# Converting the weights w1 and w2 in chunks of 1024 columns in place of 512

## The chip, the cores and the metric

The kernel runs on one core of a Trainium2 chip. The metric is the time of one execution on the device in microseconds, as the median of several runs. The engines are TensorE (PE in the profile, PEld for its weight loads), VectorE (DVE), ScalarE (ACT), GpSimd (POOL) and SyncE (SP), which here does nothing but issue transfers.

## The reference

Three blocks run one after the other on a batch of two sequences of 768 tokens and 512 features (8 heads of 64):

```python
mask = q_bucket[:, :, :, None] == k_bucket[:, :, None, :]   # buckets: signs of q @ proj, k @ proj
scores = np.where(mask, scale * q @ k.T, -1e9)
x = softmax(scores) @ v                                     # heads joined to (B, 768, 512)

u = x + np.real(np.fft.fft(np.fft.fft(x, axis=1), axis=2))
x = u + np.maximum(layernorm(u) @ w_ch1, 0.0) @ w_ch2       # 512 -> 2048 -> 512

theta = x @ w_theta
y = w_tok_r @ (x * cos(theta)) + w_tok_i @ (x * sin(theta))
u = x + y
out = u + np.maximum(u @ w_ch, 0.0)
```

The weights w_ch1, w_ch2, w_theta, w_tok and w_ch arrive as pairs of 32-bit words of float64 values.

## The kernel before

Products are formed from a high and a low part of each operand, so every weight must be converted on the core: from float64 words to float32, then into a high part (float16 for w1 and w2, fp32r for the others) and a low part, the difference.

`from_f64` does the first half for one chunk. It takes a buffer `r` from a ring of NCV = 3 in the pool `cv`, issues the load on SP, and makes float32 words of the two halves: two ScalarE operations (`r` with the bias `chalf`, then `r` again) and one VectorE operation that shifts and joins them. `conv16` (w1 and w2, 8192 columns each) and `conv32` (the theta and channel matrices `wth` and `wch`, 2048 columns each) go over the columns in chunks of CN = 512, and add two operations: ScalarE copies the chunk into the high part (`w1h`, `w2h`), GpSimd subtracts it for the low part (`w1l`, `w2l`). A buffer is free for the next load when the low part is made. `conv_tok` does the same for the token matrices in chunks of TH = 384 columns, and passes that width to `from_f64`.

The order on each engine is set by a planner: each piece of work gets a due time in us by `at(...)` (`timed` raises it by a step per chunk: w1s for w1, w2s for w2), and the planner lays the instructions in order of due time as they come ready in its own model. Each engine then runs its queue in that order. `take(cw1, k0)` and `take(cw1, k1 - k0)` part the chunks of w1 into three groups, which may start after different gates: the end of the first attention's transposes (`cv`), the first norm (`ln0`), and its last step.

Around the change the work is: the attention of the first batch (to about 136 us, order written by hand), its Fourier transform `Fft(0)` with the copies into `u` and the first norm (to about 213 us), beside it the attention of the second batch (tiles `stk`, `pss`, `p`, `pt`, `x`, 48 steps to about 375 us), and the MLP of the first batch (`psm` from `w1h`, `w1l`, then `w2h`, `w2l`). The first three chunks of w1 are loaded at the start, since their buffers are free; all other loads wait for a buffer. The same SP queue issues the transposes of the attention (`pt`, `x`). After the second attention come the transform, norm and MLP of the second batch, then theta, the token products and the channel product of both.

Of the kernel before, what the change touches and what calls it, by code (L numbers as in the profile page):

```python
# [33 lines left out]
def f(t):  # L34
    return t.bitcast(F32)
# [35 lines left out]
def fused_kernel(ctx, tc, A, out):  # L71
    nc = tc.nc
# [5 lines left out]
    def mk(p, shape, dt, tag, **kw):  # L78
        return p.tile(shape, dt, tag=tag, name=tag, **kw)
# [7 lines left out]
    def stt(eng, out, in0, in1, op, scale=1.0):  # L87
        if eng is V:
            return V.scalar_tensor_tensor(out=out, in0=in0, scalar=scale, in1=in1, op0=ALU.mult, op1=op)
        assert scale == 1.0  # L90
        return eng.tensor_tensor(out=out, in0=in0, in1=in1, op=op)

    T = dict(
        pet='dpd', dup=1, c2=0, c0=46, cx=0, wm=6, gf=1, o2=0, xs=1, sb=2, al=[['p', 2], ['p2', 3], ['pt', 3]], cs='v', g0=1,
        lg=[[0, 2], [2, 4], [4, 6]], ub=2, pace0=1.6, lead=60, f0=50.0, w1=60.0, w1s=1.0, b1=115, pace1=2.6,
        w2=100.0, w2s=1.0, m0=170.0, f1=190.0, th=240.0, m1=290.0, z0=330.0, wt=300.0, n0=8, n1=16, k0=12, k1=16, c1=46,
        ne=42, es=150, ld='ss', lc='s', ps=[[0, 3], [0, 5], [1, 0], [1, 5]])
    P3 = ((0, 0), (0, 1), (1, 0))

# [58 lines left out]
    x_t, u_t = {}, {}  # L158


    CN, NCV = 512, 3

    def from_f64(src, scale=1.0, n=CN):
        p = cvs[turn["cv"] % len(cvs)]
        turn["cv"] += 1
        r = mk(p, [128, 2 * CN], U32, "r64", bufs=NCV if p is cv_p else None)
        r = r[:, 0:2 * n]
        {"s": SY, "a": AC, "p": PL}[T["lc"]].dma_start(out=r, in_=src.bitcast(U32))
        lo, hi = r[:, 0:2 * n:2], r[:, 1:2 * n:2]

        AC.activation(out=lo, in_=lo, func=AF.Relu, scale=2.0 ** -29 * (1 - 2.0 ** -20), bias=c_half)

        AC.activation(out=f(hi), in_=f(hi), func=AF.Prelu, scale=scale * 2.0 ** -112, alpha=2.0 ** 32)
        V.scalar_tensor_tensor(out=lo, in0=hi, scalar=3, in1=lo, op0=ALU.logical_shift_left, op1=ALU.bitwise_or)
        return f(lo)
# [7 lines left out]
            yield  # L183

    def conv32(src, n, hi, lo):
        for i in range(n // CN):
            c = slice(CN * i, CN * i + CN)
            w = from_f64(src[:, c])
            AC.activation(out=hi[:, c], in_=w, func=AF.Copy)
            stt(PL, lo[:, c], w, f(hi[:, c]), ALU.subtract)  # L190
            yield
# [565 lines left out]
    w1, w2 = {}, {}  # L757
# [152 lines left out]
    h1, l1, c1, c2 = (ev(k) for k in ("aapap", "p", "p", "p"))  # L910
# [79 lines left out]

    wth = [mk(th_p, [128, 4, DM], F32R, f"wth{k}") for k in "hl"]
    timed(conv32(A["wth"], 4 * DM, flat3(wth[0]), flat3(wth[1])), T["th"], 2)
    zz = lambda p, tag: mk(p, [128, NT, DM], F32R, tag)
    z_t[0] = [[zz(x_p, "x"), zz(zb_p, "za")], [zz(zb_p, "zb"), zz(zb_p, "zc")]]
# [31 lines left out]
    def operands(p, q):  # L1026
        ks = mk(q, [128, 2, 4, TH], F32R, "ks" if q is xt_p else "u1")
        return mk(p, [128, 4, TH], F32, "xt"), ks[:, 0], ks[:, 1]
# [8 lines left out]
    k0 = operands(xt_p, xt_p)  # L1037
# [4 lines left out]
    wc_p = pool("wc", 1, side="right")  # L1042
    wch = [mk(wc_p, [128, 4, DM], F32R, f"wch{k}") for k in "hl"]
    timed(conv32(A["wch"], 4 * DM, flat3(wch[0]), flat3(wch[1])), t0 + 22, 1)
    xt1_p = pool("xt1", 1, side="right")
    k1 = operands(xt1_p, u1_p)
# [5 lines left out]
    k0 = operands(xt_p, xt_p)  # L1052
# [4 lines left out]
    k1 = operands(xt1_p, u1_p)  # L1057
# [107 lines left out]
```

## Time and profile before

| | |
|---|---|
| median of 3 runs | 739.85 us (738.78 to 742.93) |
| the profiled execution | 742.76 us |
| its span, first to last instruction | 741.0 us |
| mean granted clock of TensorE in it | 0.969 |
| busy: PE, PEld, DVE, ACT, POOL | 665.2, 508.2, 399.7, 376.5, 371.2 us |

Busy times are of the whole span; what one stage is worth is read from that stage. All rows below are of this one execution, and its own time is 2.91 us above the median.

A row of the windows gives a stretch and its length, for PE, PEld, DVE, ACT and POOL the busy us and, as (x...), the instructions, and then the granted clock (PEclk, 1.00 is full), the mean busy share of the 16 DMA engines and GB/s. A group by shape gives line, engine, operation, written and read tile, shape and count, then busy us and the mean in ns of one, then the idle us of the engine ahead of them with what ended it. The chain of waits is followed back from its last instruction; its rows in order of time give start and us. A row of DMA issues ends with KB each and the median us from issue to landing; a row of waits gives us in total, times, and the longest. The line number is L62 or L64 for all, a helper that records every operation, so tiles tell the rows apart.

### The profile page before, as it was taken

What the parts mean: (1) busy time and instruction counts of PE and PEld (TensorE: products, weight loads), DVE (VectorE), ACT (ScalarE), POOL (GpSimd) and SP (SyncE); (2) the same over time, 40 slices, a digit from 0 to 9 for tenths busy, and PEclk for the clock granted to TensorE, in tenths of its full rate; (3) what the DMA queues carried; (4) which work ended last, traced back from release to release, by engine and by line L of the source; (5) the groups of instructions that cost most, each with busy time, mean ns of one, the idle gap of its engine ahead of it and who ended that gap; (6) DMA issues with size and microseconds to landing.
All of it is one profiled execution on the core that took longest, in us unless ns stands there. A gap on an engine that the chain in (4) does not pass through costs nothing.

```text
span 741.0 us, 13335 instructions
## 1 busy us (share of the span) xinstructions
PE 665.2 (90%) x5354; PEld 508.2 (69%) x5354; DVE 399.7 (54%) x649; ACT 376.5 (51%) x603; POOL 371.2 (50%) x312
## 2 busy tenths in 40 slices
PE   5898898477687998999999999999999899979997
PEld 2465565355676656776786685786675798979997
DVE  1567787886898555443386671354322456352222
ACT  2555564967997878663322161354226555571010
POOL 2787887697796887785550030233213246631000
PEclk9999999899679999999999999999999999999999
DMA  9897976378899997777760252010014411551202
GB/s 346 184 173 147 156 109 143 107 182 224 206 223 214 254 213 213 137 130 123 119 191 2 29 122 44 26 47 1 0 46 147 159 40 31 173 184 44 85 1 86
DMA packets 161438, 93.69 MB, mean 126 GB/s; under 512 B 137056, under 2 KB 147552, under 8 KB 161376
## 3 DMA queue, kind: packets, MB, share of 16 engines
q1 hardware_dynamic: 159440, 86.27, 50.7%
q0 software_dynamic: 1936, 6.57, 2.5%
q8 instruction: 42, 0.69, 0.4%
q14 instruction: 20, 0.16, 0.1%
HBM read 49.82 MB, written 6.29 MB: 76 GB/s over the span
## 4 chain that ended last, share of the span: by engine, by line
PE 39%; issue 11%; POOL 11%; DMA 10%; ACT 6%; DVE 5%; SPq 0%; POOLq 0%; DVEq 0%; ACTq 0%
PE psm L62 26%; PE psf L62 10%; DMA r<-in_wtok 4%; POOL w1l L62 3%; POOL p L62 3%; ACT r L62 2%; PE pss L62 2%; DMA x<-p 2%; PE pso L62 2%; POOL pt L62 1%; DMA r<-in_w 1%; ACT stk L62 1%; DVE r L62 1%; DVE fa L62 1%; DMA r<-in_wch 1%
## 5 line engine op out<-in xcount | busy, mean ns | idle before, releaser
L62 PE MATMUL psm<-unT,w1h 128*128 128x256 f16 x768 | 130.9, 274 | 1.0 <-DVE hl L62 0.6
L62 PE MATMUL psm<-unT,w1l 128*128 128x256 f16 x384 | 105.2, 274 | 0.0
L62 DVE SCALAR_TENSOR_TENSOR r<-r 128x512 uint32<-128x512 uint32 (+1 forms) x64 | 61.8, 969 | 75.6 <-ACT r L62 67.8
L62 PEld LDWEIGHTS <-w1h 128*128 128x128 f16 (+1 forms) x774 | 75.3, 99 | 17.4 <-issue 6.1
L62 POOL TENSOR_TENSOR w1l<-r,w1h 128x384 fp32r<-128x384 f32 (+1 forms) x36 | 41.1, 1154 | 58.9 <-ACT w1h L62 58.6
L62 PEld LDWEIGHTS <-hh 128*128 128x128 f16 x384 | 37.2, 98 | 45.0 <-issue 3.4
L62 ACT ACTIVATE r<-r,chalf 128x512 uint32<-128x512 uint32 (+1 forms) x64 | 46.1, 720 | 40.7 <-DMA r<-in_wtok 19.2
L62 PE MATMUL pss<-stk 128*128 128x384 f32 x192 | 49.8, 388 | 17.5 <-ACT p L62 10.0
L62 PE MATMUL psm<-w2h,hh 128*128 128x512 f16 x192 | 59.6, 379 | 1.6 <-DVE hl L62 1.6
L64 PE MATMUL pss<-stk 64*128 64x384 f32 (+1 forms) x288 | 55.2, 469 | 6.5 <-ACT p L64 3.2
L62 DVE TENSOR_REDUCE nm<-pss 128x1 f32<-128x768 f32 x48 | 45.1, 947 | 27.4 <-PE pss L62 27.3
L62 PE MATMUL psm<-w2l,hh 128*128 128x512 f16 x192 | 59.8, 379 | 0.0
L62 PE MATMUL psm<-w2h,hl 128*128 128x512 f16 x192 | 59.6, 379 | 0.0
L62 POOL TENSOR_TENSOR p<-p,p 128x768 f16<-128x768 f32 x32 | 54.6, 1713 | 5.2 <-ACT p L62 4.3
L62 ACT ACTIVATE p<-pss,nm 128x768 f32<-128x768 f32 x48 | 42.7, 893 | 26.3 <-DVE nm L62 24.2
L64 DVE TENSOR_REDUCE nm<-pss 128x1 f32<-128x768 f32 x48 | 43.6, 950 | 19.8 <-PE pss L64 19.7
L62 DVE SCALAR_TENSOR_TENSOR hl<-psm,hh 128x512 f16<-128x512 f32 x48 | 32.8, 687 | 36.1 <-ACT hh L62 36.0
L62 PEld LDWEIGHTS pss<-stk 128*128 128x128 f32 x192 | 35.1, 208 | 23.9 <-ACT p L62 13.2
L62 ACT ACTIVATE hh<-psm 128x512 f16<-128x512 f32 x48 | 28.2, 592 | 39.8 <-PE psm L62 39.6
L62 PEld LDWEIGHTS <-w1l 128*128 128x128 f16 x384 | 37.8, 98 | 5.7 <-issue 1.3
L62 POOL TENSOR_TENSOR stk<-tt,stk 64x768 fp32r<-64x768 f32 x16 | 31.4, 1962 | 16.2 <-issue 12.9
L62 ACT ACTIVATE r<-r 128x512 f32<-128x512 f32 (+1 forms) x64 | 39.4, 615 | 0.0
(318 smaller groups left out, 1548.5 us busy)
## 6 DMA issues: line engine op xcount, KB each, us to landing
r<-in_w SPq DMA_DIRECT2D x32, 512.0 KB, 4.5
r<-in_wtok SPq DMA_DIRECT2D x24, 384.0 KB, 3.8
vr<-in_v SPq DMA_DIRECT2D x8, 390.0 KB, 3.5
stk<-stk SPq DMA_DIRECT2D x16, 192.0 KB, 3.2
xT<-xs SPq DMA_DIRECT2D x12, 256.0 KB, 2.6
xt<-xT SPq DMA_DIRECT2D x4, 768.0 KB, 5.0
out<-xt SPq DMA_DIRECT2D x8, 384.0 KB, 2.5
ct<-in_ct POOLq DMA_DIRECT2D x4, 579.0 KB, 7.7
```

Of the source, the lines that this page charges most:

```text
L62: return fn(*a, **k)
L64: self.last = fn(*a, **k)
```

## The change

w1, w2 go through chunks of 1024 columns: 8 chunks each in place of 16, a load of 1 MB in place of 512 KB, every instruction of `from_f64` and `conv16` on 1024 columns. The three buffers of the ring grow from 4 KB to 8 KB a partition, 12 KB in all. The steps of the due times double and the counts of the groups halve, so a column keeps its due time and its group. `conv32` is fixed at 512 columns and `conv_tok` stays at 384; both use a part of the larger buffers. The area that holds the descriptors of GpSimd's own transfers is set to 4096 in place of its default.

```diff
-        lg=[[0, 2], [2, 4], [4, 6]], ub=2, pace0=1.6, lead=60, f0=50.0, w1=60.0, w1s=1.0, b1=115, pace1=2.6,
-        w2=100.0, w2s=1.0, m0=170.0, f1=190.0, th=240.0, m1=290.0, z0=330.0, wt=300.0, n0=8, n1=16, k0=12, k1=16, c1=46,
+        lg=[[0, 2], [2, 4], [4, 6]], ub=2, pace0=1.6, lead=60, f0=50.0, w1=60.0, w1s=2.0, b1=115, pace1=2.6,
+        w2=100.0, w2s=2.0, m0=170.0, f1=190.0, th=240.0, m1=290.0, z0=330.0, wt=300.0, n0=8, n1=16, k0=6, k1=8, c1=46,
...
-    CN, NCV = 512, 3
+    CN, NCV = 1024, 3
...
     def conv32(src, n, hi, lo):
-        for i in range(n // CN):
-            c = slice(CN * i, CN * i + CN)
-            w = from_f64(src[:, c])
+        for i in range(n // 512):
+            c = slice(512 * i, 512 * i + 512)
+            w = from_f64(src[:, c], n=512)
...
-    nc = _bacc.Bacc("TRN2", target_bir_lowering=False, num_devices=1)
+    nc = _bacc.Bacc("TRN2", target_bir_lowering=False, num_devices=1, dynamic_dma_scratch_size=4096)
```

## Rows read from the trace of the kernel before

**Rows 1.** Windows: four stages, then a stretch of the last one

```profile
130.00:212.00 82.00, 54.04 (x474) 43.08 (x475) 66.33 (x109) 69.54 (x113) 64.16 (x46) 0.80 0.74 184
212.00:290.00 78.00, 68.86 (x638) 48.24 (x637) 52.47 (x72) 62.28 (x94) 60.65 (x43) 0.99 0.99 231
290.00:375.00 85.00, 81.79 (x901) 62.67 (x899) 36.74 (x53) 44.33 (x57) 56.10 (x39) 1.00 0.72 125
375.00:741.00 366.00, 352.94 (x2143) 287.55 (x2140) 162.40 (x295) 133.91 (x247) 95.31 (x98) 0.99 0.25 73
400.00:426.00 26.00, 26.00 (x157) 19.06 (x155) 14.85 (x38) 5.36 (x13) 0.00 (x0) 1.00 0.17 21
```

**Rows 2.** Tile w2l on GpSimd, ns min/median/max, first and last start

```profile
L62 POOL TENSOR_TENSOR w2l<-r,w2h x16: 1153/1172/1715, 213.3 to 278.4; 128x512 f16<-128x512 f32 x16
```

**Rows 3.** The chain of waits, 130 to 290 us, shares by line

```profile
by line: issue 20.1%; POOL p L62 11.1%; POOL w1l L62 8.8%; ACT r L62 8.0%; DMA r<-in_w 6.5%; ACT stk L62 5.9%; DVE r L62 5.2%; POOL pt L62 5.2%; POOL u L62 3.3%; ACT p L62 3.1%; POOL w2l L62 3.0%; DVE u L62 2.7%; PE psm L62 2.6%; DMA x<-p 2
```

**Rows 4.** Groups by shape, 136 to 290 us, ScalarE and VectorE

```profile
L62 ACT ACTIVATE r<-r,chalf 128x512 uint32<-128x512 uint32 x35 | 26.7, 763 | 13.3 <-DMA r<-in_w 11.5 <-POOL p L62 1.8
L62 ACT ACTIVATE r<-r 128x512 f32<-128x512 f32 x35 | 23.1, 661 | 0.0
L62 ACT ACTIVATE w1h<-r 128x512 f16<-128x512 f32 x16 | 10.4, 660 | 0.6 <-DVE r L62 0.5
L62 DVE SCALAR_TENSOR_TENSOR r<-r 128x512 uint32<-128x512 uint32 x35 | 43.1, 1235 | 30.1 <-ACT r L62 26.7 <-POOL p L62 3.1 <-issue 0.2
```

**Rows 5.** Groups by shape, whole span, ScalarE, the narrow forms

```profile
L62 ACT ACTIVATE r<-r,chalf 128x384 uint32<-128x384 uint32 x24 | 15.5, 647 | 19.6 <-DMA r<-in_wtok 19.2
L62 ACT ACTIVATE r<-r 128x384 f32<-128x384 f32 x24 | 13.0, 540 | 0.0
L62 ACT ACTIVATE w1h<-r 128x384 fp32r<-128x384 f32 x20 | 10.8, 545 | 4.0 <-DVE r L62 2.0 <-PE psm L62 1.9
```

**Rows 6.** The chain of waits from 136 us, in order of time

```profile
136.79 3.67 ACT r L62 x6
140.49 0.90 ACT stk L62
...
144.14 0.50 ACT x L64
...
152.23 3.41 POOL w1l L62 x3
155.64 1.74 POOL p L62
```

**Rows 7.** Groups by shape, GpSimd, 290 to 375 us

```profile
L62 POOL TENSOR_TENSOR p<-p,p 128x768 f16<-128x768 f32 x16 | 26.2, 1647 | 4.9 <-ACT p L62 4.3
```

**Rows 8.** Tile r on VectorE: the whole span, then 136 to 290 us

```profile
L62 DVE SCALAR_TENSOR_TENSOR r<-r x64: 547/693/3601, 138.1 to 667.3; 128x512 uint32<-128x512 uint32 x40, 128x384 uint32<-128x384 uint32 x24
...
L62 DVE SCALAR_TENSOR_TENSOR r<-r x35: 652/871/3601, 138.1 to 289.8; 128x512 uint32<-128x512 uint32 x35
```

**Rows 9.** DMA issues, the whole span, then 0 to 30 us

```profile
r<-in_w SPq DMA_DIRECT2D x32, 512.0 KB, 4.5
...
r<-in_w SPq DMA_DIRECT2D x3, 512.0 KB, 6.9
ct<-in_ct POOLq DMA_DIRECT2D x2, 579.0 KB, 8.6
```

**Rows 10.** Timeline of GpSimd, first and last early load, next split

```profile
8.85 0.59 POOL L62 DMA_DIRECT2D ct<-in_ct  x1
...
12.05 0.56 POOL L62 DMA_DIRECT2D alt<-in_alt  x1
...
19.65 0.82 POOL L64 TENSOR_SCALAR p<-p 128x768 f16<-128x768 f32 x1 [7.04 <-ACT p L64]
```

**Rows 11.** The chain of waits from 290 to 375 us, shares by line

```profile
by line: PE psm L62 37.4%; PE pss L62 14.3%; PE pso L62 11.2%; DMA x<-p 10.4%; POOL p L62 6.7%; DMA pt<-pt 6.5%; DMA pt<-p 5.8%; issue 3.7%; POOL pt L62 3.0%; DVE x L62 0.7%; POOL tt L62 0.5%; DVE r L62 0.4%; POOLq L62 0.1%; SPq L62 0.0%
```

**Rows 12.** Waits of SP, 130 to 290 us

```profile
SPq L62 <- POOL w1l L62: 27.1, 15, 5.6
```

## The prediction

> **What bounds the kernel now.** I read the windows by stage first, then the chain of waits, then the groups of the lines that the change touches. The windows [rows 1] show a kernel that TensorE sets after 290 us: it is busy for 81.8 of 85 us and then 352.9 of 366. Between 130 and 290 us it is not: 122.9 of 160 us (54.04 and 68.86), and in the first of these two windows at a granted clock of 0.80. In that stage ScalarE is busy for 131.8 us, GpSimd for 124.8, VectorE for 118.8, the DMA engines 0.74 and then 0.99: nobody is full, they wait for each other. This is where w1 and w2 are converted: the 32 low parts go from 152.2 us to 278.4 us [rows 2, 6]. The chain of the stage [rows 3] names five links of the conversion: w1l and w2l on GpSimd (8.8% and 3.0%), r on ScalarE (8.0%), the load of r (6.5%), r on VectorE (5.2%), 31.5% of 160 us or 50.4 us. So the conversion is on the path; what is saved on it can be worth something, but only here.
>
> **The change, part by part.**
> *Counts.* 32 chunks of 512 columns become 16 of 1024: 16 loads, 48 ScalarE, 16 VectorE and 16 GpSimd instructions go, and each that stays does twice the columns. The theta and channel matrices stay at 512, the token matrices at 384, the ring at three buffers: nothing after 290 us is cheaper or dearer by itself. The factors w1s, w2s, k0 and k1 move with the chunk, so a column keeps its due time and its gate.
>
> *ScalarE.* The same operations at 512 and 384 columns [rows 4, 5] part a fixed cost from a cost per column: r with the bias 763 and 647 ns, so 0.906 ns a column and 299 ns fixed; the second r 661 and 540, 177 fixed; the high part 660 and 545, 200 fixed (its narrow form writes another type, so this one is rough). Together 676 ns for each chunk that goes, 10.8 us in all. But neighbours overlap: six r operations take 3.67 us [rows 6] where their means add up to 4.27, 0.12 us a piece; with that the saving is 0.32 us a chunk, 5.1 us. On the chain r is 12.8 us; 10% to 17% of it goes, 1.3 to 2.2; I take 1.5.
>
> *GpSimd.* The low part has a median of 1172 ns at 512 columns [rows 2]; a subtraction of 768 columns takes 1647 where little disturbs it [rows 7]; 1.86 ns a column, 222 fixed, so 2.12 us at 1024. 222 of the 2344 ns of a pair, 9.5% of the 18.9 us on the chain: 1.8 us.
>
> *VectorE.* Undisturbed, r takes 652 ns at 512 and 547 at 384 columns [rows 8], 232 fixed. In the stage its mean is 1235 ns [rows 4], 583 more, and single ones take up to 3.6 us: it stands against GpSimd's operations. If a wait is paid per instruction, a pair of chunks saves 232 + 583 of 2470 ns, 33%; if it grows with the length of the blockers and of r itself, only 9%. On the chain's 8.3 us that is 0.8 to 2.7; most blockers (p, pt, stk) keep their length, so I take 2.0. The Trainium skill, SBUF — State Buffer, section Who interferes with whom, says that a VectorE instruction with two SBUF inputs and a GpSimd instruction that reads SBUF exclude each other, and that the loser stands until the whole instruction of the other is over. By that a low part of 2.12 us blocks twice as long as one of 1.17, the wait per r rises, and the term would be nearer to 0.8, the sum some 1 us worse; the maximum of 3.6 us in the trace fits the rule.
>
> *Loads.* One of 512 KB lands after a median of 4.5 us; three issued together, 1.5 MB, after 6.9 [rows 9]. One of 1 MB is not in the trace: it lies between, near 5.7, against 9.0 for two in turn. The chain's 10.4 us of loads could so lose 0 (the waits stay as long) to 5.2 (half as many waits, each as long); I take 2.5, since ScalarE can only begin when a whole chunk has landed. The Trainium skill, DMA: Bandwidth & Descriptors, section Anatomy of one DMA, gives for a load that GpSimd issues 2.0 us fixed and the bytes over 436 GB/s: 3.2 us for 512 KB and 4.4 for 1 MB as an estimate. The measured 4.5 is above that; by the page's fixed part a pair saves 2.0 of 6.4 us, and the term would be 3.3 instead of 2.5.
>
> *Order.* The first three chunks lie loaded long before they are used. Their r operations fill ScalarE from 136.79 to 140.46 us, all on the chain, with the evictions to stk (140.49) and x (144.14) queued behind them, and for x waits GpSimd with the copies into u [rows 6]. Longer by 3 x (464 + 484) ns this is 2.8 us later. The same again on GpSimd at 152.23: three low parts, 3.41 us, ahead of the p of the second attention, 2.9 us more. This is work brought forward, not added. Both in full would be 5.7 us, none 0; I take one of them, 2.9, because the planner may draw one of the evictions ahead.
>
> *The first loads.* 1.5 MB more are issued near 7 us. Three loads of 512 KB landed after 6.9 us there [rows 9], so the DMA engines can be busy up to 6.9 us longer, into the first transposes. I take 0: attention reads a transposed tile four steps after it is made, and GpSimd waits for nothing of it. If that cover were gone it would cost up to those 6.9 us once; 735.0 and 6.9 is still inside the range.
>
> *GpSimd's own loads.* Their descriptor area shrinks from its default to 4096. Seven are issued back to back, 0.55 us each, from 8.85 us on [rows 10]. I take 0, see the last rival.
>
> *Sum.* 1.5 + 1.8 + 2.0 + 2.5 = 7.8 us less, 2.9 more: 4.9 less. The bounds are 11.9 less (2.2 + 1.8 + 2.7 + 5.2, no blocking) and 1.8 more (1.3 + 1.8 + 0.8 + 0 less, 5.7 more). The profiled execution took 742.76 us, 1.76 beside its span of 741.0 and 2.91 above the median of 739.85. 742.76 - 4.9 = 737.9, and on the scale of the median 735.0.
>
> **The rivals.**
> *The gain is hidden.* After 290 us the chain goes through TensorE and through the transposes of the second attention, 10.4% for x and 12.3% for pt [rows 11], not through the conversion. If the w parts come sooner, the first batch's MLP starts sooner, but the second attention need not end sooner; and from 400 to 426 us that MLP is what keeps TensorE busy for 26.00 of 26 us [rows 1] while the second batch's transform and norm run. Work drawn forward would then leave a hole there. Against it: the attention shares ScalarE and GpSimd with the conversion before 290 us. 739.85, give or take 3.
>
> *The longer pieces block.* The other side. ScalarE works in order; at the head of its queue r waits 11.5 us in the stage for loads [rows 4], and the transform's and the attention's evictions stand behind. A buffer is free only after a low part of 2.12 us, the load takes 5.7 instead of 4.5, and SP, which already stands 27.1 us for low parts of w1 with the transposes behind [rows 12], stands longer at a time. If these waits grow by half as the turn of the ring does, they cost 5.7 us more; with the upper bound of the sum, 1.8, that is 7.5: 747.4. It decides when ScalarE's wait for the loads of w1 and w2 rises from 11.5 to over 16 us. For it: DMA at 0.99 from 212 to 290 us, which leaves no reserve for a shorter landing.
>
> *The ring was the limit.* From 136.8 to 278.4 us are 142 us for 32 chunks in three buffers: 13.3 us a turn. Load 4.5, ScalarE 2.1, VectorE 1.2, GpSimd 1.2 make 9.0 [rows 2, 4, 9]; 4.3 is standing. With half as many turns conversion could end far earlier, until ScalarE's idle 28 us of the stage are used up. If nearly half of that reaches the end, 12 us, it is 728.
>
> *GpSimd's loads queue.* If four of the seven had to wait for one before them to land (8.6 us in [rows 9]), GpSimd would stand into its first split at 19.65 us, which has 7.04 us of idle time ahead [rows 10], and again near 380 us: some 5 us, 745. The Trainium skill, DMA: Bandwidth & Descriptors, section The descriptor swizzle, counts nine read and nine write descriptors on each DMA engine for a 1 MiB load that GpSimd issues, and its section Terms gives 16 bytes for one; seven loads then make about 1 KB a side, an estimate, which speaks against this rival. No run here shows it.
>
> **How the numbers follow.** The forecast has a chance of 0.45, the hidden gain 0.17, the blocking 0.27, the ring as limit 0.08, GpSimd's loads 0.03. A change of 0.5%, 3.7 us, is about what a measurement of this kernel tells from none. Of the forecast's 0.45, 0.33 lie under 736.2, so faster is 0.33 + 0.08 = 0.41; same 0.17 + 0.12 = 0.29; slower 0.27 + 0.03 = 0.30. The likeliest time is 735.0, its own range 731 to 738, the inner half of the sum's bounds (728.0 to 741.7 on the scale of the median). Cases of both signs hold most of the chance, so the range goes to both sides: 727 takes in about half of the ring case, 747 half of the blocking, and what is left out is 0.04 + 0.13 and a rest of GpSimd's case, under 0.2.
>
> **What would show it.** Right: r on ScalarE near 1.23 and 1.15 us, the low part near 2.1, r on VectorE with a mean under 1.9; loads near 5.7 us; ScalarE's waits for them below 11.5 us; the last low part of w2 before 274 us; TensorE's idle time from 130 to 290 us below 37 us, and the second attention's end earlier by as much as the span. Wrong: a mean of r on VectorE above 2.2 (the waits grow with the length), waits for loads above 16 us, x evicted after 146.5 us and all after it later by as much, or the conversion early and a hole in TensorE between 375 and 426 us.

## The result and the profile after

The changed kernel takes 749.24 us (median of 4 runs, 748.12 to 750.89), the kernel before 740.66 on the same chip (738.78 to 742.93; one run more than in the table above). The ratio is 1.0116, with a 95% interval of 1.008 to 1.0153: slower by about 1.2%. The profiled execution has a span of 747.9 us, 6.9 more than before, and a mean granted clock of 0.951 (before 0.969). The forecast was 735.0, with 727 to 747.

First the windows of the changed kernel, cut as in [rows 1] (start and end, length, busy time of PE, PEld, DVE, ACT and POOL with the count of instructions, granted clock, DMA share, GB/s).

```profile
130.00:212.00 82.00, 56.23 (x484) 46.86 (x481) 60.88 (x86) 68.15 (x89) 64.61 (x38) 0.78 0.72 188
212.00:290.00 78.00, 65.68 (x567) 44.82 (x567) 51.87 (x78) 54.23 (x66) 51.71 (x31) 0.92 0.87 193
290.00:375.00 85.00, 84.51 (x919) 64.78 (x918) 36.18 (x52) 48.01 (x60) 58.80 (x42) 1.00 0.73 130
375.00:741.00 366.00, 354.85 (x2185) 289.11 (x2184) 164.24 (x296) 134.40 (x248) 96.32 (x99) 0.99 0.25 73
400.00:426.00 26.00, 26.00 (x146) 18.81 (x145) 15.35 (x41) 6.73 (x15) 0.00 (x0) 1.00 0.00 1
```

From 212 to 290 us TensorE runs 567 matmuls in place of 638, ScalarE is busy for 54.2 us in place of 62.3, GpSimd for 51.7 in place of 60.7, and DMA falls from 0.99 to 0.87. Less work is done in the same time, and no engine got fuller. These are the groups by shape of 136 to 290 us on ScalarE, to be read against [rows 4] (busy us, mean ns of one, idle us before them and what ended it):

```profile
L62 ACT ACTIVATE r<-r,chalf 128x1024 uint32<-128x1024 uint32 x16 | 19.8, 1240 | 7.7 <-DMA r<-in_w 7.6
L62 ACT ACTIVATE r<-r 128x1024 f32<-128x1024 f32 x16 | 18.2, 1136 | 0.0
L62 ACT ACTIVATE w2h<-r 128x1024 f16<-128x1024 f32 x8 | 8.9, 1134 | 3.7 <-DVE r L62 3.7
```

The next lines are VectorE in the same stretch, then tile w2l on GpSimd (ns min/median/max, first and last start; against [rows 2]), then the loads:

```profile
L62 DVE SCALAR_TENSOR_TENSOR r<-r 128x1024 uint32<-128x1024 uint32 x16 | 32.1, 2015 | 12.9 <-ACT r L62 7.9 <-POOL w2l L62 2.0 <-issue 1.7
...
L62 POOL TENSOR_TENSOR w2l<-r,w2h x8: 2117/2158/2593, 219.2 to 263.3; 128x1024 f16<-128x1024 f32 x8
...
r<-in_w SPq DMA_DIRECT2D x16, 1024.0 KB, 6.5
```

The pieces cost about what the prediction gave them, ScalarE waits less for loads (7.6 us, before 11.5), and conversion ends 15.1 us sooner (last low part of w2 at 263.3, before 278.4). Yet the second attention's last x (on VectorE, from pso) is at 381.0 us, before 374.5: 6.5 us later. Here is that tile from 350 to 420 us, before and then after (last start at the end of the range):

```profile
L62 DVE TENSOR_TENSOR x<-pso,r x2: 557/558/559, 356.8 to 374.5; 128x384 f32<-128x384 f32 x2
L62 DVE TENSOR_TENSOR x<-pso,r x2: 557/558/558, 361.9 to 381.0; 128x384 f32<-128x384 f32 x2
```

What lies behind it takes as long as before: 741.0 - 374.5 = 366.5 us before, 747.9 - 381.0 = 366.9 after. So the delay is there when the second attention ends. The chain from 290 to 375 us, against [rows 11], goes more over TensorE itself now and less over transposes:

```profile
by line: PE psm L62 49.5%; PE pss L62 20.7%; PE pso L62 14.0%; POOL p L62 5.9%; DMA x<-p 4.5%; issue 3.2%; DVE nm L62 1.1%; ACT p L62 1.1%; DVE x L62 0.5%; DVE r L62 0.4%; POOL pt L62 0.1%; POOLq L62 0.0%; ACTq L62 0.0%
```

psm is what the MLP writes; its share rises from 37.4% to 49.5%, so the attention now stands more behind the MLP. Finer windows say when TensorE loses. Before, then after, columns as above:

```profile
210.00:250.00 40.00, 34.87 (x345) 27.42 (x342) 34.56 (x53) 31.21 (x48) 32.71 (x22) 0.96 1.04 226
250.00:290.00 40.00, 35.99 (x304) 21.80 (x304) 19.91 (x25) 33.07 (x49) 29.86 (x23) 1.00 0.93 237
290.00:330.00 40.00, 37.26 (x445) 31.10 (x443) 21.72 (x29) 28.55 (x38) 31.85 (x22) 1.00 0.79 142
...
420.00:440.00 20.00, 19.63 (x171) 17.12 (x169) 16.76 (x53) 10.77 (x21) 4.21 (x4) 1.00 0.57 100
```

```profile
210.00:250.00 40.00, 31.53 (x290) 26.52 (x290) 33.18 (x61) 33.25 (x40) 29.60 (x17) 0.91 0.92 221
250.00:290.00 40.00, 35.48 (x297) 19.64 (x296) 19.22 (x18) 22.98 (x29) 24.11 (x15) 0.91 0.83 166
290.00:330.00 40.00, 40.00 (x472) 33.33 (x471) 20.14 (x29) 28.17 (x36) 32.46 (x24) 1.00 0.84 151
...
420.00:440.00 20.00, 16.84 (x117) 12.71 (x115) 19.31 (x67) 8.57 (x18) 3.80 (x3) 0.91 0.39 99
```

A window's length, less TensorE's busy time multiplied by the granted clock, is what the window lacks of full work. From 210 to 290 us that is 6.5 + 4.0 = 10.5 us before and 11.3 + 7.7 = 19.0 after; from 290 to 330 it is 2.7 and 0; from 420 to 440 it is 0.4 and 4.7. These are the two places: 8.5 us lost around 250 with 2.7 given back behind, and 4.3 in a hole near 430. Of the 8.5 us less than half is idle time (9.1 us before, 13.0 after); the rest is the lower mean clock, 0.91 in both windows where it was 0.96 and 1.00. The difference is larger than the scatter: two kernels below that keep the order of before (the area and the buffers alone; the pieces of 768 alone) lack 11.8 and 12.1 us there, those with late first loads and small first chunks, both slow, 19.0 and 18.3. The hole is a wait of 3.2 us for the transposed norm of the second batch (unT by DMA). Its first transpose starts at 426.8 us, before at 420.7: 46 us behind the second attention's end in both. These are the transposes from 400 to 460 us, before and after, and the changed kernel's wait:

```profile
L62 SPq DMA_TRANSPOSE unT<-u x6: 1232/1288/2331, 420.7 to 445.7; - x6
L62 SPq DMA_TRANSPOSE unT<-u x6: 1231/1244/2232, 426.8 to 445.1; - x6
...
PE psm L62 <- DMA unT<-u: 3.2, 1, 3.2
```

The second attention's pace shows in its maxima nm on VectorE, one for each of its 48 steps (the second number, in brackets, is the count). Before and then after:

```profile
212.00:250.00 38.00, 6.22 (x7) 0.99 1.04 225
250.00:290.00 40.00, 6.98 (x8) 1.00 0.93 237
290.00:350.00 60.00, 16.02 (x17) 1.00 0.74 130
```

```profile
212.00:250.00 38.00, 5.66 (x6) 0.93 0.92 223
250.00:290.00 40.00, 5.74 (x6) 0.91 0.83 166
290.00:350.00 60.00, 15.96 (x17) 1.00 0.76 139
```

That is 12 steps in place of 15 from 212 to 290 us, and they are not caught up behind it.

### The profile page after: what moved, and what is told of

Its sections match the earlier page's. It is cut to its first block, busy times and chain, and to the rows that moved or that the text cites. A ratio compares the mean times of both kernels' runs of the same rounds, so it can differ in the third digit from the quotient of the medians.

```text
span 747.9 us, 13178 instructions
## 1 busy us (share of the span) xinstructions
PE 674.2 (90%) x5354; PEld 516.0 (69%) x5354; DVE 393.5 (53%) x633; ACT 370.6 (50%) x555; POOL 366.2 (49%) x296
## 4 chain that ended last, share of the span: by engine, by line
PE 44%; issue 11%; POOL 10%; DMA 9%; ACT 4%; DVE 3%; SPq 0%; POOLq 0%; DVEq 0%; ACTq 0%
PE psm L62 30%; PE psf L62 10%; DMA r<-in_wtok 4%; POOL p L62 3%; PE pss L62 3%; PE pso L62 2%; POOL w1l L62 2%; ACT r L62 2%; DMA x<-p 2%; DVE r L62 1%; POOL stk L62 1%; POOL w2l L62 1%; DMA r<-in_wch 1%; POOL pt L62 1%; POOL u L62 1%
## 5 line engine op out<-in xcount | busy, mean ns | idle before, releaser
L62 DVE SCALAR_TENSOR_TENSOR r<-r 128x384 uint32<-128x384 uint32 (+2 forms) x48 | 54.2, 1135 | 66.9 <-ACT r L62 55.2
L62 POOL TENSOR_TENSOR w1l<-r,w1h 128x384 fp32r<-128x384 f32 (+1 forms) x28 | 39.1, 1413 | 56.3 <-ACT w1h L62 56.3
L62 PE MATMUL psm<-w2h,hh 128*128 128x512 f16 x192 | 61.2, 384 | 4.1 <-DVE hl L62 4.1
L64 PE MATMUL pss<-stk 64*128 64x384 f32 (+1 forms) x288 | 58.4, 492 | 5.9 <-ACT p L64 3.0
L62 PE MATMUL pss<-stk 128*128 128x384 f32 x192 | 51.6, 397 | 12.5 <-ACT stk L62 7.3
L62 ACT ACTIVATE r<-r,chalf 128x384 uint32<-128x384 uint32 (+2 forms) x48 | 41.5, 864 | 39.2 <-DMA r<-in_wtok 22.0
L62 PE MATMUL psm<-w2h,hl 128*128 128x512 f16 x192 | 60.7, 385 | 0.0
L62 PEld LDWEIGHTS pss<-stk 128*128 128x128 f32 x192 | 36.7, 214 | 15.7 <-ACT stk L62 8.2
L62 POOL TENSOR_SCALAR nn<-nn 128x512 f32<-128x512 f32 x12 | 7.9, 658 | 59.4 <-ACT nn L62 59.4
```

The costliest lines, as they stand in the source:

```text
L62: return fn(*a, **k)
L64: self.last = fn(*a, **k)
```

## The experiments

Each kernel ran against the kernel before on the same chip; the ratio is to that, with its 95% interval. The end of the second attention that is given with a run is that of its one profiled execution; for w2 alone wide, the last five held and the first three spread that was the slowest of its series. The theories come in three rounds. A: the start costs the time (first loads and first burst of conversion). B: the longer pieces and turns of the ring block. C: the descriptor area and the moved buffers. Then D, conversion drawn forward in the order, against E, the length of the pieces. Then F, the order of TensorE, against G, the burst of three chunks of w2 in a row.

Two series are needed that come from the program and not from a trace. The planner writes a fixed order of instructions for each engine. Where the second attention makes the high and low parts of p and pt, call an instruction on GpSimd a split. Counted from the first low part of w1, 15 18 21 23 26 28 32 32 splits stand ahead of the end of the first, second, ... eighth 1024 columns of w2l before, and 16 16 16 19 20 21 23 25 after: three parts in a row at the start, and the rest sooner. In TensorE's order, this much of the first batch's MLP (us at the full clock) stands ahead of the scores of a step of the second attention:

```
step           16  18  20  22  24  26  28  32  36  40  44
before         11  18  24  29  39  44  45  54  61  66  75
after          10  25  30  35  42  45  47  55  64  74  82
```

**The area and the buffers alone.** Edit to the kernel before:

```diff
-        r = mk(p, [128, 2 * CN], U32, "r64", bufs=NCV if p is cv_p else None)
+        r = mk(p, [128, 4 * CN], U32, "r64", bufs=NCV if p is cv_p else None)
...
+    ..., dynamic_dma_scratch_size=4096)
```

> Chunks of 512 columns, due times and order on every engine as before; only the buffers have 8 KB (half of it unused) and the descriptor area is 4096. Theory A (the start: 1.5 MB more in the first loads, and the first three chunks' longer operations ahead of x and of the second attention): as before, 740.7 within 2. Theory B (the ring's longer turn between 150 and 290 us): as before too. Theory C (the smaller descriptor area or the moved tiles): near 749.

742.80 us, 1.0013 (0.9984 to 1.0041). Buffers and GpSimd's descriptor area cost nothing that this measures; C falls, and with it the prediction's rival of GpSimd's loads.

**The first loads late.** The changed kernel with its first three loads behind the third load of v:

```diff
...
+    gate["cv"] = gate["cv"] + [gate["v2"]]
```

> The changed kernel, its first three loads of 1 MB issued behind the third load of v (near 60 us) in place of 7 us; order on all other engines the same. A: the first attention ends 1.4 to 2.7 us sooner than in the changed kernel (139.5 us), x is evicted as much sooner, and the time is 746.5 to 748. B and C: 749, no change. If the loads now collide with transposes near 62 us, the gain is lost there.

750.72 us, 1.0124 (1.0087 to 1.016): as slow as the changed kernel. Moved to 61 to 66 us, the loads that stood near 7 us change nothing.

**The first four chunks of w1 small.** The changed kernel, w1 in 4 x 512 and then 6 x 1024:

```diff
-    cw1 = conv16(A["w1"], 4 * DFF, w1[0], w1[1], pick(c1))
+    cw1 = conv16(A["w1"], 4 * DFF, w1[0], w1[1], pick(c1), (512, 512, 512, 512))
...
```

> The changed kernel with the first four chunks of w1 at 512 columns and all others at 1024, so that the first loads (1.5 MB) and the first burst are those of the kernel before. A: x evicted near 144.1 us, the first low parts take 3.4 us in place of 6.4, the time 740 to 743. B: 747 to 749, since nearly all turns of the ring are still long.

750.11 us, 1.0128 (1.0068 to 1.0189). The copies into u begin at 143.2 us in place of 150.0, x is evicted at 142.6 in place of 149.1, and the second attention still ends at 381.8. The burst at 137 us is real but does not set the end; A falls.

**w2 alone, w1 alone wide.** The changed kernel, one of the two in chunks of 512:

```diff
-    def conv16(src, n, hi, lo, lo_eng):
-        for i in range(n // CN):
+    def conv16(src, n, hi, lo, lo_eng, m=CN):
+        for i in range(n // m):
...
```

> w1 in chunks of 512 as before, w2 alone in chunks of 1024; 8 KB buffers and the small area. Order as before up to 200 us. A: 737 to 741, since the start is that of the kernel before, and half of the shorter conversion is left. B: near 745, half of the loss. C: near 749.

> w1 in chunks of 1024 columns, w2 in 512: the first half of the change alone. 33 splits of the second attention stand among the low parts, as before the change. Theory D: 740 to 744 us. Theory E: half of the loss, 744 to 747. The counterpart with w2 alone wide took 746.75.

w2 wide: 746.75 us, 1.0073 (1.0041 to 1.0104), second attention ended at 382.0. w1 wide: 739.61 us, 0.9965 (0.9936 to 0.9993), ended at 374.8. Wide chunks of w1 cost nothing; the loss comes with w2. The splits ahead of w2 are 15 16 18 21 22 23 25 26 with w2 wide and 15 20 21 24 25 28 31 33 with w1 wide. With w2 wide no three parts stand in a row, and it is slow all the same; ahead of step 40 it has 74 us of MLP, the kernel with w1 wide 64.

**Six buffers of 4 KB.** The kernel before with `CN, NCV = 512, 6`: the bytes in flight and nearly the order of the changed kernel (16 16 16 21 21 21 23 25), all pieces short.

> Chunks of 512 columns as before, but six buffers of 4 KB in place of three, so the same bytes in flight as after the change; all pieces short. In the order of GpSimd's work 25 splits (p and pt) of the second attention then stand between the first low part and the last, as after the change, in place of 32. Theory D, that the loss comes from conversion work drawn forward ahead of the second attention: 747 to 751 us, last w part before 270 us, second attention ended near 381. Theory E, that the loss comes from the length of the pieces (a longer r and low part stand in front of attention's work): 739 to 743 us, second attention ended near 375.

739.92 us, 0.9981 (0.9956 to 1.0007), but the second attention ended at 383.8. By the total D misses; by the end of the second attention it holds: only 739.1 - 383.8 = 355.3 us lie behind, 11 less than in the two kernels of the case. Six buffers bring the token matrices sooner too; this run mixes two effects, taken apart below.

**Wide loads, short operations.** The changed kernel, each 1 MB load worked on in two halves:

```diff
+            if i % 2 == 0:
+                r = load16(src[:, 512 * i:512 * i + 1024])
+            w = words(r[:, 1024 * (i % 2):1024 * (i % 2) + 1024], 512, 2.0)
...
```

> Loads of 1024 columns as after the change, but each operation (both r, high part, or, low part) in two halves of 512. The order has 25 splits of the second attention among the low parts, as after the change. Theory D (drawn forward): 747 to 751 us. Theory E (length of the pieces): 740 to 744. If only the size of the loads mattered: as after the change too, so this run is read beside the one with six buffers.

747.03 us, 1.0073 (1.0041 to 1.0105), second attention ended at 382.4. Most of the loss stays with short pieces while the order stays (15 15 15 18 21 21 23 25); that they help a little is neither shown nor excluded, since its interval and that of the changed kernel overlap. And r on VectorE stands just as long in it with 512 columns, up to 5.8 us (136 to 290 us):

```profile
L62 DVE SCALAR_TENSOR_TENSOR r<-r x35: 676/693/5794, 138.1 to 276.8; 128x512 uint32<-128x512 uint32 x35
```

**The changed kernel, w2 paced.** The eight chunks of w2, still 1024 wide, each held behind a step of the second attention:

```diff
+                    if n in steps:          # 8, 11, 13, 15, 17, 19, 21, 22
+                        gate["step"] = m + [sp]
+                        with after_gate(0), after_gate("step"):
+                            for _ in range(steps.count(n)):
+                                next(conv)
```

> The changed kernel with the eight chunks of w2 each held behind one step of the second attention, so that the splits ahead of each 1024 columns of w2 are 15 17 20 22 25 29 32 32, near those of before (15 18 21 23 26 28 32 32) and not those of after (16 16 16 19 20 21 23 25). Pieces stay 1024 wide. Theory D: 739 to 744 us, second attention ended near 375. Theory E: 747 to 751, ended near 381.

740.21 us, 0.998 (0.9958 to 1.0003); second attention ended at 372.8. The whole loss is gone with every piece as wide as in the changed kernel. E falls. The windows show the hole near 430 gone and the other place mended in part: from 210 to 290 us 14.5 us lack, where it was 10.5 before and 19.0 in the changed kernel. The kernel with wide loads and short operations, which is slow, lacks 14.7 us there, so this place alone does not tell a slow kernel from a fast one. The windows are followed by x on VectorE, as above:

```profile
210.00:250.00 40.00, 30.16 (x301) 24.29 (x301) 32.14 (x58) 32.65 (x41) 33.07 (x19) 0.87 0.92 212
250.00:290.00 40.00, 39.25 (x337) 25.61 (x335) 21.05 (x24) 32.31 (x39) 33.38 (x21) 1.00 1.01 223
420.00:440.00 20.00, 20.00 (x168) 16.67 (x168) 18.03 (x55) 12.46 (x24) 5.11 (x4) 1.00 0.54 131
...
L62 DVE TENSOR_TENSOR x<-pso,r x2: 557/558/558, 354.5 to 372.8; 128x384 f32<-128x384 f32 x2
```

**Which chunks of w2.** The same edit, once for the last five chunks alone, once spread over the first three with the others nearly free:

```diff
-steps=(8, 11, 13, 15, 17, 19, 21, 22)
+steps=(15, 17, 19, 21, 22)                 # last five held, first three free
...
+steps=(8, 11, 13, 13, 13, 13, 13, 15)      # first three spread
```

> The changed kernel with only the last five chunks of w2 held: splits ahead of each 1024 columns of w2 16 16 16 23 26 29 32 32, so the three low parts in a row of the changed kernel stay and the rest is as in the paced run (740.21). Theory D in the form that the mean pace decides: 739 to 742 us. In the form that the three low parts in a row (6.5 us at 219 us) with the normalisation behind them decide: 745 to 750.

> The changed kernel with the first three chunks of w2 spread and the others nearly free: 15 17 21 21 24 25 25 28, between the changed kernel (16 16 16 19 20 21 23 25; 749.2) and the paced one (740.2). By mean pace 743 to 746 us; if the three in a row decide, 739 to 742.

Last five held: 750.11 us, 1.011 (1.0077 to 1.0144), second attention ended at 382.2. First three spread: 741.66 us, 0.9998 (0.9966 to 1.0031), ended at 367.9. So the mean pace does not decide. The first three chunks could, but w2 alone wide was slow without three in a row; or what the planner writes with them does: with the last five held 72 us of MLP stand ahead of step 40, with the first three spread 63. In each of the slow kernels so far it is 72 to 74, and in each that is as fast as before 63 to 66, but for the six buffers (72, with the second attention late and time gained elsewhere). An early end of the second attention is not time saved by itself: in the run with the first three spread, 744.3 - 367.9 = 376.4 us lie behind it, 10 more than before.

**TensorE's order undone, conversion left.** The changed kernel, each unit of the first batch's MLP (2.56 us) held behind as many steps of the second attention as in the kernel before:

```diff
+            s = next(held) if not b and n < 8 else 0
+            with after_gate(gate["S"][s - 1] if s else None):
```

> The changed kernel with all conversion in its own order (splits ahead of the columns of w2 still 16 16 16 19 20 21 23 25, three low parts in a row at the start), but each unit of the first batch's MLP on TensorE (2.56 us, 48 units) held behind as many steps of the second attention as in the kernel before: 63 us of MLP ahead of step 40 in place of 74, where before had 66. Theory F, that the loss lies in the order of TensorE (the planner puts the MLP ahead of the second attention, which then ends late and leaves a hole near 430 us): second attention ended near 375, no hole near 430, 739 to 744 us. Theory G, that the three low parts in a row and the r and high parts that belong to them cost the time themselves: 747 to 751, second attention near 381.

745.90 us, 1.0045 (1.0011 to 1.0079); second attention ended at 380.0. This lies between the two theories: some of the loss is gone, some stays. Ahead of step 40 stand 63 us of MLP.

```profile
210.00:250.00 40.00, 30.55 (x278) 25.49 (x279) 32.62 (x61) 31.66 (x40) 27.86 (x16) 0.91 0.92 229
250.00:290.00 40.00, 34.62 (x301) 20.17 (x300) 18.69 (x17) 26.86 (x33) 28.53 (x17) 0.91 0.83 171
420.00:440.00 20.00, 20.00 (x139) 14.04 (x138) 16.99 (x61) 5.68 (x13) 3.81 (x3) 1.00 0.29 76
```

The hole near 430 is closed: the first transpose of unT is again 46.8 us behind the attention's end, at 426.8, but now there is MLP left to cover it. From 210 to 290 us nothing is mended: 12.2 + 8.5 = 20.7 us lacking.

**TensorE's order made, without the wide chunks.** The kernel before, 512 columns, with steps of the second attention held behind units of the MLP about as the changed kernel has them:

```diff
+                    for _ in range(steps.count(n)):
+                        next(units)
+                    with after_gate("unit" if n in steps else None):
+                        ps = attn_S(st[hh], t)
```

> The kernel before, chunks of 512 columns and its order of conversion nearly kept (26 27 28 30 splits ahead of the last four 1024 columns in place of 26 28 32 32), but the steps of the second attention held behind the units of the first batch's MLP about as in the changed kernel: 31 36 41 45 49 56 64 72 81 us of MLP ahead of steps 20 to 44 (every second up to 28, then every fourth), where the changed kernel has 30 35 42 45 47 55 64 74 82 and before 24 29 39 44 45 54 61 66 75. Theory F: 745 to 751 us, second attention ended near 381, a hole near 430. Theory G: 740 to 743.

750.31 us, 1.0107 (1.0065 to 1.0149); second attention ended at 382.2, first transpose of unT at 428.5. With the order of TensorE made so, short chunks cost what the change costs, with a larger hole (a wait of 6.3 us). From 210 to 290 us this kernel lacks 15.3 us. TensorE has to obey the added edges, which may cost time by themselves; no run adds edges that keep the order of before, though those of the paced kernel, on conversion, cost nothing.

```profile
PE psm L62 <- DMA unT<-u: 6.3, 1, 6.3
...
420.00:440.00 20.00, 13.68 (x90) 10.08 (x89) 17.81 (x65) 8.02 (x17) 3.80 (x3) 0.83 0.39 104
```

**Behind 560 us.** Six buffers with w2 paced as above; the paced wide kernel with the token matrices in pieces of 768 in place of 384 columns; the kernel before with those pieces (and buffers of 8 KB) alone:

```diff
-            w = from_f64(A["wtok"][half][:, TH * n:TH * n + TH], n=TH)
+            w = from_f64(A["wtok"][half][:, TH * n:TH * n + 2 * TH], n=2 * TH)
...
```

> Six buffers of 4 KB and chunks of 512 as in the run with six buffers (739.92 us, second attention ended at 383.8), but with w2 held behind the steps of the second attention, so that the splits ahead of each 1024 columns of w2 are 15 16 19 22 25 29 32 32 in place of 16 16 16 21 21 21 23 25. Theory D (work drawn forward delays the second attention, and the six buffers gave that run back some 10 us behind 560 us, where the token matrices come sooner): second attention ended near 375, 729 to 734 us. If the order of w2 were worth nothing with short pieces: 739 to 741.

> The paced run with wide chunks (740.21) and the token matrices in pieces of 768 columns in place of 384 as well, so that a ring of three buffers holds six of their old pieces. If the run with six buffers gained behind 560 us by having the token matrices sooner: 729 to 735 us, the idle times of TensorE near 590 and 670 us gone. If it gained by something else: 738 to 742.

> The kernel before in its own order, chunks of 512 columns in buffers of 8 KB used by half, and the token matrices in pieces of 768 columns in place of 384. The paced kernel with wide chunks gained 6.7 us by these pieces (740.2 to 733.5). If that gain has nothing to do with the chunks of w1 and w2: 733 to 737 us, TensorE's idle times near 590 and 670 us gone. If wide chunks, once paced, are themselves worth something, this stays 2 us or more above 733.5.

734.58 us, 0.9898 (0.9855 to 0.9941); 733.48 us, 0.9879 (0.9834 to 0.9925); 734.94 us, 0.9897 (0.9855 to 0.9939). With six buffers, pacing takes the second attention's end from 383.8 to 375.3 us and 5.3 us off the time, with short pieces: D's order again. In all three TensorE's idle times near 590 and 670 us are gone or nearly so. The kernel before, then the one with the pieces of 768 alone:

```profile
580.00:600.00 20.00, 17.84 (x89) 16.19 (x88) 10.31 (x17) 9.56 (x17) 4.99 (x6) 0.91 0.30 104
660.00:680.00 20.00, 17.63 (x93) 17.31 (x92) 4.34 (x8) 5.76 (x12) 4.42 (x5) 0.91 0.37 117
```

```profile
580.00:600.00 20.00, 20.00 (x111) 18.68 (x110) 10.25 (x18) 10.64 (x19) 6.21 (x8) 1.00 0.14 41
660.00:680.00 20.00, 19.53 (x113) 19.53 (x113) 3.35 (x6) 1.58 (x3) 0.42 (x1) 1.00 0.12 40
```

That gain needs no wide chunk of w1 or w2: the intervals of 734.94 and 733.48 us overlap. Both are faster than the kernel before by about 1%.

## Why the prediction was wrong

*The step that failed* is one sentence of the counts: that the factors move with the chunk, "so a column keeps its due time and its gate", and with it the sum's premise that outside the start the order stays. The due times are not what sets this order here: with w2=125, w2s=3.0 in place of 100 and 2.0, 25 to 32 us later, the changed program is the same, instruction by instruction; it was not run by itself. What holds conversion back is the ring of three buffers; with twice the columns in a buffer the planner lets three chunks of w2 follow each other at once, draws the rest of w2 forward, and fills TensorE with MLP ahead of the second attention. The prediction looked at order only at the start and priced it at 2.9 us; there it cost nothing that reaches the end (the first four chunks small: 750.11 us).

*What took its place.* That the order costs the time and not the length of the pieces is shown: in a good order wide pieces cost nothing (w2 paced, 0.998), and a bad order costs with short ones too (1.0107 with added edges; 1.0073 without them, the loads alone wide). Within the order there are two effects, each seen in a run in which the other is held off by edges. Conversion drawn forward: 12 steps of attention in place of 15 from 212 to 290 us, some 8 to 10 us of TensorE lost from 210 on, part of it given back (with TensorE's order undone, the kernel keeps it and is 0.45% slow, interval 0.11% to 0.79%). TensorE's order: with the MLP drawn forward and short chunks, 1.07% slow. They don't add: each alone makes the second attention end at 380 to 382 us, and both together at 381. Without both (w2 paced) it is 372.8. How much of either the edges themselves cost is not shown. What also stays open is how much of the first effect belongs to the burst of three and how much to the dense chunks behind it: with the burst kept and the last five held, 210 to 290 us lack 12.3 us, near the 10.5 of before, and that kernel's loss sits in the hole (72 us of MLP ahead of step 40). Nor did a run try the burst alone, with both other orders as before.

*Point by point.* ScalarE's r at 1240 and 1136 ns (expected 1.23 and 1.15 us), the low part at 2.1 to 2.2 us, and ScalarE's wait for loads of 7.6 us were right; the loads at 6.5 us were above the 5.7 expected. VectorE's r has a mean of 2015 ns, between the two bounds (1.9 and 2.2): the pair saves 18% and not 33% of 2470. In the paced kernel it is 1645, so this term depends on what stands beside it. The saving is on the chain of 130 to 290 us: the five links of conversion, 31.5% in [rows 3], are 24.3% after (r on VectorE 6.1, r on ScalarE 5.8, w2l 4.9, loads 4.1, w1l 3.4). It did not reach the end, because the attention did not take the room. One sign of being wrong came, x evicted after 146.5 us (149.1), but it is not the cause: in the paced kernel x is evicted at 151.8 us and the time is that of before. First r on VectorE from 136 to 290 us in the paced kernel, then the chain of the changed kernel:

```profile
L62 DVE SCALAR_TENSOR_TENSOR r<-r 128x1024 uint32<-128x1024 uint32 x16 | 26.2, 1645 | 6.9 <-ACT r L62 5.1 <-POOL p L62 1.2 <-POOL w2l L62 0.6
...
by line: issue 21.1%; POOL p L62 9.9%; DVE r L62 6.1%; POOL stk L62 6.0%; ACT r L62 5.8%; POOL w2l L62 4.9%; POOL pt L62 4.7%; POOL u L62 4.2%; DMA r<-in_w 4.1%; PE psm L62 3.9%; POOL w1l L62 3.4%; ACT p L62 3.1%; DMA x<-p 2.9%; DMA pt<-pt 
```

*The rivals.* "The longer pieces block" had 747.4, near the time, but by the wrong cause: its condition, waits for loads over 16 us, did not come (7.6), and wide pieces, paced, cost nothing. "The gain is hidden" named the mechanism that came, conversion early and a hole in TensorE, but placed it at 375 to 426 us, took it for neutral, and did not see that the second attention would end later. The hole lies at 420 to 440. The two small rivals are out: GpSimd's loads with the small area cost nothing (the area and the buffers alone, 1.0013), and the ring was a limit, but one that kept a good order.

## What to carry to other kernels

A buffer ring is also a brake on the planner. Whoever widens it should compare the order of every engine, above all of the one that is the bound, before costing instructions: here the instructions got cheaper, nearly as computed, and the kernel slower. A step that must not run ahead is held by an edge to the work it should follow; due times 25 to 32 us later did not do it. And where one long stage ends in a fixed chain (46 us from the second attention's end to the first transposed norm), count what the bound engine still has in hand for it.

## What the runs showed of the hardware

A VectorE instruction stood through three GpSimd instructions in a row. In the changed kernel r of 1024 columns on VectorE begins at 250.56 us and takes 5.75, where [rows 8] give an estimate of 1.1 for its own work (0.82 ns a column from 652 and 547 ns, and 232 ns fixed). GpSimd meanwhile runs w2l, p and pt back to back until 255.22, and r ends 1.1 us behind them. The eviction hl comes after it, at 256.23, and a matmul of the MLP waits 4.11 us for that (timelines of VectorE, GpSimd and TensorE):

```profile
250.56 5.75 DVE L62 SCALAR_TENSOR_TENSOR r<-r 128x1024 uint32<-128x1024 uint32 x1 [3.01 <-ACT r L62]
256.23 0.68 DVE L62 SCALAR_TENSOR_TENSOR hl<-psm,hh 128x512 f16<-128x512 f32 x1
...
249.90 2.14 POOL L62 TENSOR_TENSOR w2l<-r,w2h 128x1024 f16<-128x1024 f32 x1
251.99 1.64 POOL L62 TENSOR_TENSOR p<-p,p 128x768 f16<-128x768 f32 x1
253.59 1.63 POOL L62 TENSOR_TENSOR pt<-p,pt 128x768 f16<-128x768 f32 x1
...
256.96 0.59 PE L62 MATMUL psm<-w2h,hh 128*128 128x512 f16 x1 [4.11 <-DVE hl L62]
```

The rule of the Trainium skill cited in the prediction (SBUF — State Buffer, section Who interferes with whom) lets the loser stand until the whole instruction of the other is over; here it was three of them, two of which convert nothing. With pieces of 512 columns r stands as long (5794 ns above), so the longest stand does not come from the length of the low part. The prediction read the maximum of 3.6 us before as a sign that a longer low part would block for longer; that r, too, stands through p and pt, back to back, and ends 0.55 us behind them, with no low part among them:

```profile
244.73 3.60 DVE L62 SCALAR_TENSOR_TENSOR r<-r 128x512 uint32<-128x512 uint32 x1 [1.76 <-ACT r L62]
...
244.54 1.64 POOL L62 TENSOR_TENSOR p<-p,p 128x768 f16<-128x768 f32 x1
246.14 1.64 POOL L62 TENSOR_TENSOR pt<-p,pt 128x768 f16<-128x768 f32 x1
```

In the changed kernel the two un of the norm, at 221.32 us, stand in the three low parts in a row, 4.70 us for the pair (the shortest un there takes 0.53 us), and there each waits for about one:

```profile
219.22 6.51 POOL L62 TENSOR_TENSOR w2l<-r,w2h 128x1024 f16<-128x1024 f32 x3
...
221.32 4.70 DVE L62 TENSOR_SCALAR un<-u,mv,rs 128x512 f32<-128x512 f32 x2
```

That is one way in which conversion drawn forward slows the work beside it, seen in the trace and not tried by itself.
